# LSH attention and a mixture of experts on one core: who splits the last quarter of the first w1, and how the last chunk is made

## The chip, the cores and the metric

The kernel runs on one NeuronCore of a Trainium2 chip. Its engines work side by side, each through its own queue in order: TensorE (PE; its weight loads are PEld), VectorE (DVE), ScalarE (ACT), GpSimd (POOL) and SyncE (SP), which here only issues transfers. The metric is device time of one execution in microseconds: before the change the median of three runs is 708.36 us (708.22 to 708.40).

## The reference

Attention with a mask from locality-sensitive hashing, over 4 batches of 8 heads with 768 positions of 64 numbers, and then a mixture of 8 experts that sends each of the 3072 tokens to one of them:

```
q_bucket = sum((q @ proj > 0) * 2**arange(6));  k_bucket likewise
scores   = where(q_bucket == k_bucket, q @ k.T / 8, -1e9)
attn     = exp(scores - max) / (sum + 1e-9)
x        = attn @ v                      # as 3072 x 512
e        = argmax(x @ w_gate)            # one expert for a token
h        = relu(x[e] @ w1[e])            # 512 -> 1024
out      = softmax(x @ w_gate)[e] * sigmoid(x @ w_output_gate)[e] * (h @ w2[e])
```

All is float32. To keep its precision on TensorE, operands are split in two parts of the type fp32r, a rounded copy (`hi`) and what the copy leaves (`lo`), and a product is the sum of three matmuls: hi with hi, hi with lo, lo with hi.

## The kernel before

The work has two parts. The **attention part** goes through 192 steps of one tile of scores (128 queries, 768 keys in a folded layout). For a step TensorE makes the scores (line 555), VectorE takes the masked minimum (line 558), ScalarE makes exponentials and their sums (line 566), VectorE the reciprocal for a pair of steps (lines 573 and 574), GpSimd multiplies by it (line 576: the normalisation), TensorE transposes the result in twelve pieces (line 600), ScalarE and VectorE copy these out of PSUM (lines 602 and 606), and TensorE multiplies with v (line 617). A tile is transposed six steps after its scores, so that the engines have time; the last six steps (186 to 191) are transposed in a loop that makes no scores any more.

The **expert part** runs expert after expert, largest first. For an expert, `up` (line 329) makes `h` from gathered tokens, a column block `f` at a time, with ScalarE writing `hh` (line 337) and VectorE `hl` (line 338). Then `h @ w2` is made, for the last experts in rows: `all_rows` makes a chunk of at most 128 tokens by 24 matmuls of 512 columns into one PSUM bank, `ps_m` for even chunks and `ps_a` for odd ones. `send` scales it by the gate into `yo` and scatters its rows to the output with an indirect transfer of GpSimd. The last chunk of the last expert has 96 tokens. For this one `send` lets ScalarE scale the first half of the columns and VectorE the second.

The two parts overlap for the first expert, whose number is known before the last batch ends. Its first 256 tokens are gathered from the batches that are done, turned by TensorE into `ps_m` (a pool with one buffer, lines 279 to 284) and brought out by ScalarE (`xh`, line 283) and VectorE (`xlo`, line 284). Its w1 comes in four quarters of 128x1024 through two buffers named `w_raw`; `early_w1` splits each in two halves on GpSimd (line 938 `hi`, line 939 `lo`). Then eight fills, one for each `f`, are laid among the routing of the last batch; w2 comes in four pieces, two through `w_raw` and two through the idle buffer `pts0`, split by GpSimd (line 179) and VectorE (line 182).

What is issued where is set by tables. `plan(step, fn)` puts `fn` behind the transposes of a step; `late` is step 168, so that the entry 20 for a half of w1 means step 188 and 22 step 190. The queues of TensorE, VectorE, ScalarE and GpSimd follow the order of the program in the two blocks under `manual_schedule`, in the first block SyncE too; where two blocks meet, a scheduler lays small instructions of both between each other. The lines of the table before:

```
for h in range(2):
    plan(late + (8, 10, 13, 14, 16, 19, 20, 22)[2 * cc + h], lambda cc=cc, h=h: early_w1(cc, h))
```

SyncE issues, in this order: the stores of attention rows to `x_dram` (line 636, which wait for VectorE's transposition on line 629), the first two w2 pieces into `w_raw` (line 172, each once that buffer's w1 quarter is split), and the two pieces into `pts0` (line 162).

Of the kernel before, what the change touches and what calls it, by code (L numbers as in the profile page):

```python
# [8 lines left out]
F32 = mybir.dt.float32  # L9
# [4 lines left out]
AF = mybir.ActivationFunctionType  # L14
ALU = mybir.AluOpType
# [9 lines left out]
DM = H * D  # L25
E = 8
# [3 lines left out]
CH = P  # L30
# [13 lines left out]
NCC = DM // P  # L44
GROUP = 2
PER = 6
NFB = F // P
# [7 lines left out]
def f32(ap):  # L55
    return ap.bitcast(F32)
# [3 lines left out]
def lsh_attention_then_moe(  # L60
# [10 lines left out]
    nc = tc.nc  # L71
# [53 lines left out]
    tacc_e, tacc = (cst.tile([CH, 3, E, NCH], F32, name=n) for n in ("tacc_e", "tacc"))  # L125
# [197 lines left out]
    def product(ps, ls, rs, first=True, last=True):  # L323

        pairs = [p for (lh, ll), (rh, rl) in zip(ls, rs) for p in ((lh, rh), (lh, rl), (ll, rh))]
        for k, (l, r) in enumerate(pairs):
            nc.tensor.matmul(ps, l, r, start=first and k == 0, stop=last and k == len(pairs) - 1)  # L327
# [12 lines left out]
    def send(r, a, n, py, sid):  # L340

        yo = mp.tile([CH, DM], F32, name="yo", bufs=4)
        gt = tacc[0:n, 1, r, a:a + 1]
        m = DM // 2 if (r, a) == (E - 1, len(chunks(r)) - 1) else DM
        nc.scalar.activation(yo[0:n, 0:m], py[0:n, 0:m], AF.Copy, scale=gt)  # L345
        if m < DM:
            nc.vector.tensor_scalar(yo[0:n, m:DM], py[0:n, m:DM], gt, None, ALU.mult)
        nc.gpsimd.indirect_dma_start(  # L348
            out=out[:, :], out_offset=bass.IndirectOffsetOnAxis(ap=sid[0:n, r, a:a + 1], axis=0),
            in_=yo[0:n], in_offset=None, bounds_check=NTOK - 1, oob_is_err=False)  # L350
# [25 lines left out]
    def all_rows(r, a, c, n, w2s, hs, sid, between):  # L376
        py = (ps_a if a % 2 else ps_m).tile([CH, DM], F32, name="ps_a" if a % 2 else "ps_m")
        for f in range(0, NFB, 2):
            down_rows(c, n, w2s, hs, py, [f, f + 1])
            between()  # L380
        send(r, a, n, py, sid)

    def chunks(r):

        return [min(CH, CAPS[r] - c) for c in range(0, CAPS[r], CH)]

    with ExitStack() as actx:
# [22 lines left out]
        def plan(step, *fns):  # L410
            at.setdefault(step, []).extend(fns)
# [416 lines left out]
        for b in range(B - 1):  # L828
            r = routing(b)
# [102 lines left out]
        def early_w1(cc, h):  # L932
            if h == 0:
                early.setdefault("w1", []).append(
                    [wpool.tile([P, F], F32R, name="w1" + n, bufs=NCC) for n in "hl"])
            c = slice(h * F // 2, (h + 1) * F // 2)
            hi, lo, raw = (x[:, c] for x in (*early["w1"][cc], early["raw"][cc]))
            nc.gpsimd.tensor_scalar(hi, raw, 1.0, 0.0, ALU.mult, ALU.add)
            nc.gpsimd.tensor_tensor(lo, raw, f32(hi), ALU.subtract)

# [5 lines left out]
        for cc in range(NCC):  # L946
            plan(late + (4, 5, 11, 15)[cc], lambda cc=cc: early_load(cc))
            for h in range(2):
                plan(late + (8, 10, 13, 14, 16, 19, 20, 22)[2 * cc + h], lambda cc=cc, h=h: early_w1(cc, h))

        with tc.manual_schedule(engines=MANUAL | {mybir.EngineType.SP}):
            t = signs()
# [130 lines left out]
    with tc.manual_schedule(engines=MANUAL):  # L1083
# [18 lines left out]
        for r in range(E):  # L1102
# [73 lines left out]
            if n > 3 * CH:  # L1176
                back = [mp.tile([P, 2, CAP], F32, name="yt", bufs=2) for _ in range(NCC // 2)]
                for dp in range(NCC // 2):
                    down(w2s, hs, n, back, dp, between)
            else:  # L1180
                back = None
                c0 = 0 if r else EARLY
                for a in range(c0, len(ch)):
                    all_rows(r, a, a - c0, ch[a], w2s, hs, sid, between)
            split()
            if nxt:
                w1s, xs = w1n, xn
# [109 lines left out]
```

## Time and profile before

| | |
|---|---|
| median of three runs | 708.36 us |
| profiled execution | 708.33 us |
| its span | 706.5 us |
| TensorE busy | 691.4 us, 98% |
| VectorE, ScalarE, GpSimd busy | 466.1, 439.9, 396.7 us |
| chain that ended last | TensorE 91%, VectorE 5% |

Times in the rows below are microseconds from the start of the span. A busy time counts an engine's own instructions; what stands in brackets behind an instruction is the idle time of its engine just before it, and what ended it. Matmuls are pipelined: the duration of one is longer than the distance to the next, and the distance is what counts. An engine that is idle costs something only where another waits for it.

### The profile page before, as it was taken

How to read it: one execution, taken by the hardware profiler on the slowest of the kernel's cores; microseconds unless marked ns; L12 is line 12 of the kernel's file. 1: busy time of each engine (PE TensorE's matmuls, PEld its weight loads, DVE VectorE, ACT ScalarE, POOL GpSimd, SP SyncE). 2: the span in 40 equal slices, each digit the busy share in tenths (PEclk: the TensorE clock that was granted, in tenths of full speed). 3: DMA queues.
4: the chain of work that ended last, by engine and by line, in shares of the span. 5: the costliest groups of instructions: out<-in, count | busy, mean ns of one | idle time of the engine just before them, and what ended most of it. 6: DMA issues, size and time to landing. Idle time of an engine off the chain costs nothing.

```text
span 706.5 us, 17341 instructions
## 1 busy us (share of the span) xinstructions
PE 691.4 (98%) x6591; PEld 543.1 (77%) x6591; DVE 466.1 (66%) x1045; ACT 439.9 (62%) x896; POOL 396.7 (56%) x489
## 2 busy tenths in 40 slices
PE   7999999999999999999999999999999999999996
PEld 4666675767675767675766889889999999989894
DVE  7787887888777888778975944462636455555440
ACT  5789988889788888888887213423425243434231
POOL 6668666575756566656699246344372727474201
PEclk9999999999999999999999999999999999999999
DMA  5544554444444544442535225633454453636401
GB/s 177 142 122 98 122 124 108 116 89 107 116 118 85 117 102 124 86 109 60 144 84 142 54 91 181 218 107 122 163 166 158 163 168 115 215 122 212 152 9 43
DMA packets 85283, 87.47 MB, mean 124 GB/s; under 512 B 57167, under 2 KB 67591, under 8 KB 85192
## 3 DMA queue, kind: packets, MB, share of 16 engines
q1 hardware_dynamic: 79704, 72.88, 37.7%
q0 software_dynamic: 5200, 13.31, 5.5%
q8 instruction: 54, 0.88, 0.5%
q14 instruction: 37, 0.30, 0.2%
q10 hardware_dynamic: 288, 0.10, 0.1%
HBM read 59.57 MB, written 13.11 MB: 103 GB/s over the span
## 4 chain that ended last, share of the span: by engine, by line
PE 91%; DVE 5%; issue 1%; ACT 1%; DMA 1%; POOL 0%; POOLq 0%; DVEq 0%; ACTq 0%
PE ps_s L327 32%; PE ps_a L617 18%; PE ps_s L555 17%; PE ps_t L600 6%; PE ps_m L327 6%; PE ps_a L327 3%; DVE sc L558 2%; PE ps_t L447 1%; PE ps_m L600 1%; PE ps_a L600 1%; PE ps_m L651 1%; PE ps_t L241 1%; DVE w2l L182 1%; PE ps_a L367 0%; PE ps_m L367 0%
## 5 line engine op out<-in xcount | busy, mean ns | idle before, releaser
L576 POOL TENSOR_SCALAR sc<-sc,rsum 128x768 f32<-128x768 f32 x192 | 171.3, 908 | 121.9 <-ACT pts L606 62.9
L558 DVE TENSOR_SCALAR_CACHE_REDUCE sc<-ps_s 128x768 f32<-128x768 f32 x192 | 176.3, 954 | 22.0 <-PE ps_s L555 20.3
L566 ACT ACTIVATE sc<-sc,mn 128x768 f32<-128x768 f32 x192 | 178.8, 951 | 3.7 <-DVE sc L558 3.6
L555 PE MATMUL ps_s<-kh,qhl 64*128 64x384 f32 x768 | 150.5, 404 | 2.3 <-DVE sc L558 1.6
L617 PE MATMUL ps_a<-pts,vt 128*64 128x384 f32 x768 | 131.1, 490 | 0.0
L606 ACT COPY pts<-ps_t 128x384 f32<-128x384 f32 x189 | 93.2, 493 | 34.2 <-PE ps_s L600 27.8
L338 DVE SCALAR_TENSOR_TENSOR hl<-ps_s,hh 128x256 fp32r<-128x256 f32 (+8 forms) x40 | 34.0, 849 | 105.8 <-ACT hh L337 105.8
L617 PEld LDWEIGHTS ps_a<-pts,vt 128*64 128x64 f32 x768 | 52.2, 137 | 66.5 <-issue 61.8
L600 PEld LDWEIGHTS ps_t<-ident,sc 64*128 64x128 f32 x1152 | 83.7, 140 | 20.9 <-POOL sc L576 12.9
L327 PE MATMUL ps_s<-xh,w1h 128*128 128x256 f32 (+7 forms) x288 | 96.8, 336 | 0.0
L327 PE MATMUL ps_s<-xlo,w1h 128*128 128x256 f32 (+7 forms) x288 | 95.3, 331 | 0.0
L348 POOL DMA_INDIRECT out_dram<-yo,sid x29 | 31.0, 1068 | 114.4 <-ACT yo L345 56.8
L327 PE MATMUL ps_s<-xh,w1l 128*128 128x256 f32 (+7 forms) x288 | 95.1, 330 | 0.0
L301 POOL DMA_INDIRECT xq<-x_dram,idx x75 | 81.3, 1084 | 23.8 <-issue 21.1
L600 PE MATMUL ps_t<-ident,sc 64*128 64x64 f32 x1152 | 88.6, 225 | 0.7 <-POOL sc L576 0.7
L337 ACT ACTIVATE hh<-ps_s 128x256 fp32r<-128x256 f32 (+8 forms) x40 | 29.1, 727 | 96.0 <-PE ps_s L327 96.0
L555 PEld LDWEIGHTS ps_s<-kh,qhl 64*128 64x128 f32 x768 | 77.1, 189 | 4.7 <-DVE sc L558 2.8
L555 PE MATMUL ps_s<-bb 64*128 64x384 bf16 x384 | 65.8, 329 | 2.7 <-DVE sc L558 1.6
L555 PE MATMUL ps_s<-kl,qhl 64*128 64x384 f32 x384 | 66.9, 334 | 0.0
L606 ACT COPY pts<-ps_m 128x384 f32<-128x384 f32 x93 | 44.7, 480 | 18.0 <-PE ps_m L600 12.9
L327 PEld LDWEIGHTS ps_s<-xh,w1h 128*128 128x128 f32 x288 | 54.1, 188 | 2.0 <-issue 0.6
L327 PEld LDWEIGHTS ps_s<-xlo,w1h 128*128 128x128 f32 x288 | 54.1, 188 | 1.3 <-DVE xlo L284 0.2
(228 smaller groups left out, 1376.0 us busy)
## 6 DMA issues: line engine op xcount, KB each, us to landing
w_raw<-in_w_dram SPq DMA_DIRECT2D x34, 512.0 KB
qk<-in_qkT_dram SPq DMA_DIRECT2D x32, 384.0 KB
qhl<-qhl SPq DMA_DIRECT2D x62, 192.0 KB
xh<-in_w_dram SPq DMA_DIRECT2D x14, 512.0 KB
xlo<-in_w_dram SPq DMA_DIRECT2D x14, 512.0 KB
vt<-in_v_dram SPq DMA_DIRECT2D x16, 384.0 KB
x_dram<-xb SPq DMA_DIRECT2D x60, 96.0 KB
xq<-x_dram,idx POOLq DMA_INDIRECT x75, 2.8
```

The source lines that it names most:

```text
L301: nc.gpsimd.indirect_dma_start(out=xq[:, k * P:(k + 1) * P], out_offset=None, in_=x_dram.rearrange("n (a f) -> (n a) f", a=NB32), in_offse ...
L327: nc.tensor.matmul(ps, l, r, start=first and k == 0, stop=last and k == len(pairs) - 1)
L337: nc.scalar.activation(hh, ph, AF.Relu)
L338: return lambda: nc.vector.scalar_tensor_tensor(hl, ph, 0.0, f32(hh), ALU.max, ALU.subtract)
L348: nc.gpsimd.indirect_dma_start(out=out[:, :], out_offset=bass.IndirectOffsetOnAxis(ap=sid[0:n, r, a:a + 1], axis=0), in_=yo[0:n], in_offse ...
L555: nc.tensor.matmul(ss[:, h, 0:HS], q[rs, c:c + P], k[rs, 0:HS], start=(i == 0), stop=(i == 3))
L558: nc.vector.tensor_scalar(sc, ss[:, :, 0:HS], MASKED, None, ALU.min, ALU.min, accum_out=mn)
L566: nc.scalar.activation(pr, pr, AF.Exp, bias=mn, scale=-1.0, accum_out=sums[s // GROUP][:, k, 0:1])
L576: nc.gpsimd.tensor_scalar(live[s0 + k], live[s0 + k], rs[:, k:k + 1], 0.0, ALU.mult, ALU.add)
L600: nc.tensor.transpose(trs[h][:, c], pr[r, c * P:(c + 1) * P], ident[r, r])
L606: (nc.vector.tensor_copy if h and (last or s % PER == 0) else nc.scalar.copy)(pts[:, :, t * P + h * hq:t * P + (h + 1) * hq], trs[h])
L617: nc.tensor.matmul(st["av"][j * D:(j + 1) * D], st["v"][:, j, c], blocks[hb][j][:, c], start=(c == 0), stop=(c == NT - 1))
```

## The change

Two things are changed. In `early_w1` the last quarter (`cc == NCC - 1`) is split by VectorE instead of GpSimd, with a copy and a subtraction for each half, and both halves are planned at step 191 (`late + 23`), behind the last step with scores, instead of at 188 and 190. And the last chunk of the last expert is made by a new function, `last_rows`: the two halves of its 512 columns one after the other, the first in `ps_m` and scaled by VectorE, the second in `ps_a` and scaled by ScalarE. The scatter is a function of its own.

```diff
-        m = DM // 2 if (r, a) == (E - 1, len(chunks(r)) - 1) else DM
-        nc.scalar.activation(yo[0:n, 0:m], py[0:n, 0:m], AF.Copy, scale=gt)
-        if m < DM:
-            nc.vector.tensor_scalar(yo[0:n, m:DM], py[0:n, m:DM], gt, None, ALU.mult)
+        nc.scalar.activation(yo[0:n], py[0:n], AF.Copy, scale=gt)
+        scatter(yo, r, a, n, sid)
+
+    def scatter(yo, r, a, n, sid):
+
         nc.gpsimd.indirect_dma_start(
...
+    def last_rows(r, a, c, n, w2s, hs, sid):
+
+        m = DM // 2
+        yo = mp.tile([CH, DM], F32, name="yo", bufs=4)
+        gt = tacc[0:n, 1, r, a:a + 1]
+        cs = slice(c * CH, c * CH + n)
+        for k, (pool, name) in enumerate(((ps_m, "ps_m"), (ps_a, "ps_a"))):
+            py = pool.tile([CH, m], F32, name=name)
+            d = slice(k * m, (k + 1) * m)
+            product(py[0:n], [(hs[0][:, f, cs], hs[1][:, f, cs]) for f in range(NFB)],
+                    [(w2s[f][0][:, d], w2s[f][1][:, d]) for f in range(NFB)])
+            if k == 0:
+                nc.vector.tensor_scalar(yo[0:n, d], py[0:n], gt, None, ALU.mult)
+            else:
+                nc.scalar.activation(yo[0:n, d], py[0:n], AF.Copy, scale=gt)
+        scatter(yo, r, a, n, sid)
...
+            if cc == NCC - 1:
+                nc.vector.tensor_copy(hi, raw)
+                nc.vector.tensor_tensor(lo, raw, f32(hi), ALU.subtract)
+                return
             nc.gpsimd.tensor_scalar(hi, raw, 1.0, 0.0, ALU.mult, ALU.add)
             nc.gpsimd.tensor_tensor(lo, raw, f32(hi), ALU.subtract)
...
-                plan(late + (8, 10, 13, 14, 16, 19, 20, 22)[2 * cc + h], lambda cc=cc, h=h: early_w1(cc, h))
+                plan(late + (8, 10, 13, 14, 16, 19, 23, 23)[2 * cc + h], lambda cc=cc, h=h: early_w1(cc, h))
...
-                    all_rows(r, a, a - c0, ch[a], w2s, hs, sid, between)
+                    if (r, a) == (E - 1, len(ch) - 1):
+                        last_rows(r, a, a - c0, ch[a], w2s, hs, sid)
+                    else:
+                        all_rows(r, a, a - c0, ch[a], w2s, hs, sid, between)
```

What the change does to the queues is seen in their order. First GpSimd at the end of the attention part, before: the normalisations of the last eight steps (`sc`), the gathers of tokens (`xg`), the last three halves of w1 and the copies for w2.

```order
L576 TENSOR_SCALAR sc<-sc,rsum 128x768 x4
L269 DMA xg<-x_dram,gid_7560 128x512 x2
L938 TENSOR_SCALAR w1h<-w_raw 128x512
L939 TENSOR_TENSOR w1l<-w_raw,w1h 128x512
L938 TENSOR_SCALAR w1h<-w_raw 128x512
L939 TENSOR_TENSOR w1l<-w_raw,w1h 128x512
L576 TENSOR_SCALAR sc<-sc,rsum 128x768 x2
L938 TENSOR_SCALAR w1h<-w_raw 128x512
L939 TENSOR_TENSOR w1l<-w_raw,w1h 128x512
L576 TENSOR_SCALAR sc<-sc,rsum 128x768 x4
L179 TENSOR_SCALAR w2h<-w_raw 128x1024 x2
L179 TENSOR_SCALAR w2h<-pts_7869 128x1024 x2
```

And GpSimd in the same place of the changed kernel, whose line numbers are higher by up to 22:

```order
L594 TENSOR_SCALAR sc<-sc,rsum 128x768 x4
L269 DMA xg<-x_dram,gid_7560 128x512 x2
L960 TENSOR_SCALAR w1h<-w_raw 128x512
L961 TENSOR_TENSOR w1l<-w_raw,w1h 128x512
L594 TENSOR_SCALAR sc<-sc,rsum 128x768 x6
L179 TENSOR_SCALAR w2h<-w_raw 128x1024 x2
L179 TENSOR_SCALAR w2h<-pts_7869 128x1024 x2
```

Two halves are gone, and the last six normalisations stand together. Next VectorE in the same place, before: the last four minima (`sc,mn`), the sums and reciprocals of the last three pairs, and the transposition of attention rows (`xb`) between them.

```order
L558 TENSOR_SCALAR sc,mn<-ps_s 128x768 x4
L573 TENSOR_REDUCE rsum<-terms 128x2
L574 RECIPROCAL rsum<-rsum 128x2
L629 STREAM_TRANSPOSE xb<-ot 128x384
L573 TENSOR_REDUCE rsum<-terms 128x2
L574 RECIPROCAL rsum<-rsum 128x2
L573 TENSOR_REDUCE rsum<-terms 128x2
L574 RECIPROCAL rsum<-rsum 128x2
```

The same place on VectorE in the changed kernel:

```order
L576 TENSOR_SCALAR sc,mn<-ps_s 128x768 x4
L591 TENSOR_REDUCE rsum<-terms 128x2
L592 RECIPROCAL rsum<-rsum 128x2
L957 CAST w1h<-w_raw 128x512
L958 TENSOR_TENSOR w1l<-w_raw,w1h 128x512
L957 CAST w1h<-w_raw 128x512
L958 TENSOR_TENSOR w1l<-w_raw,w1h 128x512
L647 STREAM_TRANSPOSE xb<-ot 128x384
L591 TENSOR_REDUCE rsum<-terms 128x2
L592 RECIPROCAL rsum<-rsum 128x2
L591 TENSOR_REDUCE rsum<-terms 128x2
L592 RECIPROCAL rsum<-rsum 128x2
```

The four new instructions stand ahead of the transposition and of the sums of the last two pairs. Third, VectorE later, among the fills: before, from the fifth `hl` to the sixth, with the ranks and places of the last batch (`t_ge`, `t_oa`, `t_na`, `t_pos`, `t_rhs`) and the order of the experts (`perm`, `o_place`, `o_tm`).

```order
L893 SCALAR_TENSOR_TENSOR o_key<-lead,o_key 128x8
L338 SCALAR_TENSOR_TENSOR hl<-ps_s,hh 128x256
L202 TENSOR_TENSOR t_ge<-rank,chki 128x30
L894 TENSOR_TENSOR perm<-o_key 128x64
L205 TENSOR_TENSOR t_oa<-t_ge 128x24
L211 TENSOR_REDUCE t_na<-t_ge 128x6
L897 TENSOR_REDUCE o_place<-perm 128x8
L213 SCALAR_TENSOR_TENSOR t_pos<-t_na,rank 128x6
L226 TENSOR_TENSOR t_rhs<-oneh,t_oa 128x192
L898 TENSOR_TENSOR perm<-o_place,rkdi 128x64
L230 TENSOR_TENSOR t_rhs<-t_rhs,toki 128x192
L230 TENSOR_TENSOR t_rhs<-t_rhs,gate 128x192
```

The instruction behind these is the sixth `hl`. The same place in the changed kernel, from `perm` on, which there stands ahead of the fifth `hl`:

```order
L912 TENSOR_TENSOR perm<-o_key 128x64
L338 SCALAR_TENSOR_TENSOR hl<-ps_s,hh 128x256
L202 TENSOR_TENSOR t_ge<-rank,chki 128x30
L915 TENSOR_REDUCE o_place<-perm 128x8
L205 TENSOR_TENSOR t_oa<-t_ge 128x24
L211 TENSOR_REDUCE t_na<-t_ge 128x6
L916 TENSOR_TENSOR perm<-o_place,rkdi 128x64
L213 SCALAR_TENSOR_TENSOR t_pos<-t_na,rank 128x6
L226 TENSOR_TENSOR t_rhs<-oneh,t_oa 128x192
L933 TENSOR_TENSOR o_tm<-perm,expi 128x64
L230 TENSOR_TENSOR t_rhs<-t_rhs,toki 128x192
L230 TENSOR_TENSOR t_rhs<-t_rhs,gate 128x192
```

The instructions that order the experts stand earlier, and one more of them (`o_tm`) comes ahead of the sixth `hl`. SyncE's queue has the same order as before.

## Rows read from the trace of the kernel before

**Rows 1.** Busy us by stretch (instructions), granted clock, DMA share, GB/s.

```profile
core 0: us, PE busy (x) PEld busy (x) DVE busy (x) ACT busy (x) POOL busy (x), PEclk, DMA share, GB/s
380.00:390.00 10.00, 8.96 (x110) 6.25 (x107) 4.96 (x13) 7.41 (x15) 9.92 (x11) 1.00 0.80 230
...
410.00:700.00 290.00, 290.00 (x1554) 268.50 (x1553) 134.91 (x147) 106.82 (x130) 130.13 (x131) 1.00 0.43 146
```

**Rows 2.** Timeline of GpSimd: start, us, instruction, count, idle before it.

```profile
378.78 0.61 POOL L938 TENSOR_SCALAR w1h<-w_raw 128x512 fp32r<-128x512 f32 x1
...
380.74 1.79 POOL L576 TENSOR_SCALAR sc<-sc,rsum 128x768 f32<-128x768 f32 x2
...
384.46 3.54 POOL L576 TENSOR_SCALAR sc<-sc,rsum 128x768 f32<-128x768 f32 x4
387.98 2.06 POOL L179 TENSOR_SCALAR w2h<-w_raw 128x1024 fp32r<-128x1024 f32 x2
390.80 3.19 POOL L179 TENSOR_SCALAR w2h<-pts 128x1024 fp32r<-128x1024 f32 x2 [0.76 <-DMA pts<-in_w_dram]
```

**Rows 3.** Timeline of TensorE, from the last transposes to the eighth fill.

```profile
382.82 0.79 PE L600 MATMUL ps_t<-ident,sc 64*128 64x64 f32 x12
...
385.42 0.59 PE L600 MATMUL ps_t<-ident,sc 64*128 64x64 f32 x12 [0.74 <-POOL sc L576]
386.30 0.59 PE L600 MATMUL ps_s<-ident,sc 64*128 64x64 f32 x12 [0.29 <-POOL sc L576]
386.81 0.75 PE L281 MATMUL ps_m<-ident,xg 128*128 128x128 f32 x4
...
397.29 0.85 PE L671 MATMUL ps_m<-wgt,ot 128*128 128x32 f32 x6 [0.17 <-DVE ot L620]
...
398.19 0.28 PE L327 MATMUL ps_s<-xlo,w1h 128*128 128x256 f32 x1
...
400.78 0.28 PE L327 MATMUL ps_s<-xh,w1l 128*128 128x256 f32 x1
...
405.61 0.39 PE L327 MATMUL ps_s<-xh,w1h 128*128 128x256 f32 x1
```

**Rows 4.** Timeline of VectorE in the same stretch.

```profile
380.59 0.16 DVE L573 TENSOR_REDUCE rsum<-terms 128x2 f32<-128x4 f32 x1 [2.06 <-ACT sc L566]
...
382.42 0.16 DVE L573 TENSOR_REDUCE rsum<-terms 128x2 f32<-128x4 f32 x1 [1.47 <-ACT sc L566]
...
385.35 0.69 DVE L284 TENSOR_TENSOR xlo<-ps_m,xh 128x512 fp32r<-128x512 f32 x1 [1.14 <-ACT xh L283]
...
389.53 3.55 DVE L182 TENSOR_TENSOR w2l<-w_raw,w2h 128x1024 fp32r<-128x1024 f32 x2
...
396.70 0.54 DVE L620 COPY ot<-ps_a 128x384 f32<-128x384 f32 x1
...
405.13 0.42 DVE L338 SCALAR_TENSOR_TENSOR hl<-ps_s,hh 128x256 fp32r<-128x256 f32 x1
```

**Rows 5.** VectorE's prices: one start, one line by min/median/max, one group.

```profile
4.10 0.35 DVE L472 TENSOR_SCALAR qhl<-qk 64x384 fp32r<-64x384 f32 x1 [1.91 <-DMA qk<-in_qkT_dram]
...
L182 DVE TENSOR_TENSOR w2l<-w_raw,w2h x16: 1216/1222/2054, 389.5 to 679.2; 128x1024 fp32r<-128x1024 f32 x16
...
L510 DVE SCALAR_TENSOR_TENSOR qhl<-qk,qhl 128x384 fp32r<-128x384 f32 x30 | 24.5, 816 | 4.1 <-POOL qhl L504 2.8
```

**Rows 6.** Chain that ended last, merged: start, us, line, pieces.

```profile
695.07 5.54 PE ps_m L327 x24
```

**Rows 7.** Timeline of all engines behind the last product.

```profile
700.68 0.47 ACT L345 ACTIVATE yo<-ps_m,tacc 96x256 f32<-96x256 f32 x1 [4.83 <-PE ps_m L327]
701.18 0.48 DVE L347 TENSOR_SCALAR yo<-ps_m,tacc 96x256 f32<-96x256 f32 x1 [15.53 <-ACT yo L345]
701.94 0.93 POOL L348 DMA_INDIRECT out_dram<-yo,sid  x1 [4.84 <-DVE yo L347]
```

**Rows 8.** Timeline of SyncE's transfers.

```profile
378.56 2.10 SPq L636 DMA_DIRECT2D x_dram<-xb  x4
380.90 0.36 SPq L172 DMA_DIRECT2D w_raw<-in_w_dram  x1
```

## The prediction

> **What bounds the kernel now.** I read three views, in this order. First the busy time by stretch: from 410 to 700 us TensorE is busy 290.00 of 290.00 us at full granted clock [rows 1]. So whatever reaches the end of the attention part earlier is kept to the end, and nothing can be won in that stretch except by taking work off TensorE. Between 380 and 390 us it is busy 8.96 of 10 us, and GpSimd 9.92 [rows 1]: here the attention part runs out and the experts begin. Second, the timelines of the engines in that place, to see who holds TensorE. Third, the tail, where the order of three engines behind the last product is plain.
>
> At the hand-over GpSimd holds TensorE. GpSimd makes a half of the last w1 quarter from 378.78 to 380.74, then two normalisations (1.79 us), then the second half until 384.46, and only then the four last softmax normalisations, 3.54 us for four [rows 2]. TensorE's third set of transposes of the last block starts at 385.42 after 0.74 us of waiting for GpSimd, the fourth at 386.30 after another 0.29 [rows 3]. VectorE, meanwhile, was idle 2.06 us before 380.59 and 1.47 us before 382.42 [rows 4].
>
> **Part one: the last quarter moves from GpSimd to VectorE.** GpSimd loses four instructions, two halves of 1.96 us each (378.78 to 380.74, and as much for the second) [rows 2], 3.9 us in all. VectorE gains four, two copies and two subtractions of 512 columns, between the last minima and the transposition of 0.57 us that started at about 378.0 (380.59 less 2.06 of idle time is 378.53, its end). No row shows a copy of this shape. The nearest is a scaled copy of 384 columns in 0.35 us [rows 5], so 0.47 for 512. A subtraction of 1024 columns takes 1.22 us at the median and 2.05 at most [rows 5]: 0.61 to 1.03 for half of that. The 2.05 were beside GpSimd's copies, which then took 1.60 each instead of 1.03 (3.19 for two against 2.06) [rows 2]. The same addition of 0.42 on a copy makes it 0.9. Four instructions cost VectorE 2.2 us alone and 3.9 us beside a busy GpSimd. GpSimd is busy for the first two thirds of that time, so I take 3.0: from 378.0 to 381.0. The mean of 0.82 us for another two-input instruction of 384 columns [rows 5], 1.09 for 512, agrees with the upper half.
>
> What is queued behind them on VectorE: the transposition of 0.57, then the reduction for the second last pair, which ran at 380.59 [rows 4]. It comes at about 381.6, its reciprocal at about 382.0. GpSimd is free by then (one quarter half and two normalisations from 378.78), and makes four at 0.885: the second last pair by 383.8, the last pair (its reduction at 382.42 [rows 4] is not moved) by 385.5, which was 388.0 before.
>
> TensorE's third set then starts without its 0.74, at 384.68; it lasted 0.59 (386.30 less 0.29 less 385.42), so the fourth is at 385.27, again without a wait, and the second turn of gathered rows is reached at about 385.8. It cannot start there: it writes the one ps_m bank, which the first turn's subtraction on VectorE frees at 385.35 + 0.69 = 386.04 [rows 4]. That subtraction hangs on TensorE and ScalarE, which the change does not move. With 0.05 to the start (as from 397.24 to 397.29 below) the turn begins at 386.09 instead of 386.81 [rows 3]. **Gain here: 0.72 us**, of 1.03 us of waits removed; 0.3 turn into a wait for the bank.
>
> The next place is 397.29: the products that add the last pair of heads to the logits waited 0.17 us for VectorE's copy, 396.70 + 0.54 [rows 3, 4]. That copy is queued behind four subtractions for w2 that began at 389.53 [rows 4]. If TensorE comes 0.72 earlier and VectorE were free, the gain would be 0.72 + 0.17 = 0.89. VectorE's four begin when the last transposes are copied, some 0.6 earlier. If the block keeps its length, 0.6 is all; if it is shorter, because GpSimd's w2 copies are over sooner, up to 0.89. I take 0.75, the middle.
>
> **The order of small instructions behind it.** The code there is the same, but three routing instructions of the expert order come earlier on VectorE: one more stands ahead of the sixth `hl` subtraction, and two dependent ones follow each other closely ahead of the fifth. In the trace the sixth `hl` subtraction ran at 405.13 for 0.42, to 405.55, and TensorE's eighth fill began at 405.61 [rows 3, 4], right behind it, since it takes the PSUM tile that this frees. So any delay there is TensorE's. An instruction of this size with a dependent one beside it is 0.2 to 0.25 us (the small reductions are 0.16 [rows 4], and each waits for the one before). **Cost: 0.25 us**, bounds 0 and 0.4.
>
> **Part two: the tail.** Before, 24 matmuls of 512 columns take 5.54 us [rows 6], then ScalarE scales one half in 0.47 (700.68), then VectorE the other in 0.48 (701.18), having waited for ScalarE, and GpSimd scatters at 701.94 [rows 7]. Afterwards VectorE's half is done while the second half of columns is still in TensorE, so the scatter waits for ScalarE alone: 701.66 less 701.15, 0.51 us saved. TensorE issues 48 matmuls of 256 columns. Such ones stand in the trace 22 steps apart from 398.19 to 400.78 [rows 3], 0.118 us each: 48 make 5.65, 0.11 more than 5.54. Their weights have 96 columns, in that stretch 128, so 0.118 should be no less than what comes. **Gain: 0.40 us** (0.35 to 0.5).
>
> **Sum.** 0.75 - 0.25 + 0.40 = 0.90 us. The profiled execution took 708.33 us, a span of 706.5 and 1.8 around it, and the median of three runs is 708.36. 708.33 - 0.90 = 707.4 us. The likeliest case's own range, with 0.6 to 0.89, 0 to 0.4 and 0.35 to 0.5, is 706.9 to 707.8.
>
> **A rule that speaks against the change.** The rows show VectorE and GpSimd slowing each other when both read SBUF (1.22 to 2.05 and 1.03 to 1.60 us) [rows 2, 5]. The Trainium skill, "SBUF — State Buffer", section "Who interferes with whom", says more: a VectorE copy in its two-port mode, or a VectorE instruction with two SBUF inputs against a GpSimd one that reads SBUF, shares one port pair with it as an exclusive lock, and whoever comes second is blocked until the other has finished. By that rule the new instructions and GpSimd's work add up: VectorE's 2.2, the 0.8 that GpSimd still has of the sixth half at 378.0 and two normalisations of 0.885 are 4.8, so VectorE is free at 382.8, the reciprocal at 383.8; the third set would start at about 384.9 and the turn at 386.3, 0.2 us later than I have it, and the sum would be 0.7.
>
> **The rivals.** *More is won.* The waits of TensorE between 382.82 and 397.29 [rows 3] are 1.20 us in sum. If the bank of the turn comes free sooner than the old rows say, and the shifted order costs nothing, the gain is 0.89 to 1.20 + 0.40, that is 707.0 to 706.7. For it: VectorE's queue has slack in front of the first turn, and the cost of the order is read from one release at 405.55 alone. Against it: the bank's rows hang on TensorE's own start at 382.82 [rows 3].
>
> *Only the tail pays.* If VectorE's block for w2 ends no earlier than before, the wait at 397.29 takes the place of the one at 385.42, and with the order's 0.25 part one is worth nothing or less: 0.40 - 0.25 to 0.40, 708.0 to 708.2. What could hold that block is its input, below. Against it: GpSimd is ready for the w2 copies 2.5 us earlier than at 387.98 [rows 2].
>
> *Slower.* The mechanism is SyncE's queue. Its four stores of attention rows (issued from 378.56 for 2.10 us) wait for VectorE's transposition, and the first w2 load stands behind them, at 380.90 [rows 8]. With the transposition at 381.6 they are issued until 383.7, and the first load comes at 384.0, 3.1 later. The second load was held by its buffer until about 384.5 anyway, which GpSimd freed at 384.46 [rows 2] and VectorE now frees at 381. So all four loads start together at about 384, with the stores still moving. In the trace GpSimd waited for the third piece until 390.80, 0.76 us [rows 2], so there was little slack. If the loads come so late that the last w2 subtraction ends 1.8 us later than before, the 0.40 of the tail is lost and the kernel is 1.4 us slower; from 0.4 us on it is not faster. At 3 us it is 711. Against it: the later loads need no more bytes, the transfer engines were busy only 0.80 of that stretch [rows 1], and the block may slip by 1 us before it costs more than is won. The lock of which the Trainium skill speaks would push it this way, by another 1.8 us on SyncE's stores.
>
> **How the numbers follow.** Chances: the forecast 0.55, more 0.22, only the tail 0.16, slower 0.07. What a measurement of this kernel can tell from no change is about 0.2%, 1.4 us. The forecast and most of the tail case lie inside that; the first rival reaches it only with its best values, and a few tenths that I have not seen would do the rest, so faster is 0.22, same 0.71, slower 0.07. The range, 706.6 to 708.2, takes in all but the far ends of the first rival and the slower one.
>
> **What would show it.** In the profile after: GpSimd's normalisations joined to a group of six with no w1 work between, the last ending near 385.5; no wait for GpSimd at the third and fourth set of transposes, but one of about 0.3 for VectorE or ScalarE at the second turn; the w2 subtractions ending before 395.6; the eighth fill waiting longer for its `hl`; 48 matmuls in about 5.65 us, and only ScalarE between the last of them and the scatter. It is wrong if GpSimd waits over 1.5 us for w2's pieces, if the four VectorE instructions take more than 4 us, or if the narrow matmuls are further apart than 0.12 us.

## The result and the profile after

The changed kernel is slower: 712.52 us, median of four runs (710.33 to 713.0), against 708.29 us for the kernel before (four runs, 706.97 to 708.4) measured beside it. The ratio is 1.0067, with a 95% interval of 1.0054 to 1.0081, that is 3.8 to 5.7 us. The forecast of 707.4 and its range (706.6 to 708.2) missed it, and the case that came had 7% of the chance.

The profiled execution is the fastest of the four: 710.33 us, span 708.6. Its attention part ran earlier from the start: the same products with v (line 635, line 617 before) begin here at 377.56 us, in the trace of before at 378.80. One reason stands in the rows of 10 to 30 us: granted clock 1.00 here, 0.91 there. So times of the hand-over are compared with 1.24 us added to those of the changed kernel.

SyncE after, in the columns of [rows 8]:

```profile
381.23 2.10 SPq L654 DMA_DIRECT2D x_dram<-xb  x4
383.57 1.00 SPq L172 DMA_DIRECT2D w_raw<-in_w_dram  x2
384.83 0.88 SPq L162 DMA_DIRECT2D pts<-in_w_dram  x2
```

The four stores and the first w2 load are each 2.67 us later than in [rows 8], 3.91 with the 1.24. Why the stores are late shows on VectorE (start, length, and in brackets the idle time before):

```profile
376.73 1.11 DVE L957 CAST w1h<-w_raw 128x512 fp32r<-128x512 f32 x1
377.88 1.27 DVE L958 TENSOR_TENSOR w1l<-w_raw,w1h 128x512 fp32r<-128x512 f32 x1
379.07 0.42 DVE L957 CAST w1h<-w_raw 128x512 fp32r<-128x512 f32 x1
379.52 1.19 DVE L958 TENSOR_TENSOR w1l<-w_raw,w1h 128x512 fp32r<-128x512 f32 x1
380.64 0.56 DVE L647 STREAM_TRANSPOSE xb<-ot 128x384 f32<-128x384 f32 x1
...
389.20 1.23 DVE L182 TENSOR_TENSOR w2l<-w_raw,w2h 128x1024 fp32r<-128x1024 f32 x1 [1.40 <-POOL w2h L179]
391.36 1.23 DVE L182 TENSOR_TENSOR w2l<-w_raw,w2h 128x1024 fp32r<-128x1024 f32 x1 [0.94 <-POOL w2h L179]
393.52 3.18 DVE L182 TENSOR_TENSOR w2l<-pts,w2h 128x1024 fp32r<-128x1024 f32 x2 [0.94 <-POOL w2h L179]
...
397.21 0.54 DVE L638 COPY ot<-ps_a 128x384 f32<-128x384 f32 x1
```

The four new instructions take 3.98 us (376.73 to 380.71), and the transposition for which the stores wait stands behind them. In the trace of before it ran here, 3.91 us earlier with the 1.24:

```profile
377.97 0.56 DVE L629 STREAM_TRANSPOSE xb<-ot 128x384 f32<-128x384 f32 x1
```

Further down in the trace of after VectorE waits three times for GpSimd's copies of w2, and the copy that TensorE needs starts at 397.21, 1.75 us later than in [rows 4]. GpSimd itself:

```profile
377.54 2.64 POOL L594 TENSOR_SCALAR sc<-sc,rsum 128x768 f32<-128x768 f32 x2
381.63 3.56 POOL L594 TENSOR_SCALAR sc<-sc,rsum 128x768 f32<-128x768 f32 x4 [1.46 <-DVE rsum L591]
388.12 1.04 POOL L179 TENSOR_SCALAR w2h<-w_raw 128x1024 fp32r<-128x1024 f32 x1 [2.92 <-DMA w_raw<-in_w_dram]
389.89 1.43 POOL L179 TENSOR_SCALAR w2h<-w_raw 128x1024 fp32r<-128x1024 f32 x1 [0.73 <-DMA w_raw<-in_w_dram]
392.07 2.43 POOL L179 TENSOR_SCALAR w2h<-pts 128x1024 fp32r<-128x1024 f32 x2 [0.74 <-DMA pts<-in_w_dram]
```

GpSimd is done with the normalisations at 385.19, with the 1.24 some 1.5 us earlier than in [rows 2], and then waits 2.92 us for the first w2 piece, which lands 4.55 us after its issue (383.57 to 388.12). In [rows 2] the same wait is absent, because GpSimd was still at its own work when that piece landed. The third piece comes late too, though its issue hardly moved. In the trace of before SyncE issued it here:

```profile
385.12 0.88 SPq L162 DMA_DIRECT2D pts<-in_w_dram  x2
```

With the 1.24 it is issued 0.95 us later in the changed kernel (384.83), but GpSimd begins it 2.51 later (392.07 against 390.80 [rows 2]) and ends its last copy 1.75 later. All four loads now move together, right behind the stores: from 382 to 391 us the transfer engines are busy 0.97 of the time, in the trace of before 0.71 (the last column but one; the first line is before).

```profile
382.00:391.00 9.00, 7.96 (x105) 6.07 (x103) 5.63 (x11) 5.79 (x12) 8.15 (x10) 1.00 0.71 236
382.00:391.00 9.00, 8.28 (x108) 6.26 (x109) 4.67 (x8) 4.89 (x9) 5.35 (x6) 1.00 0.97 268
```

And TensorE, from the third set of transposes on:

```profile
383.52 0.59 PE L618 MATMUL ps_t<-ident,sc 64*128 64x64 f32 x12
383.94 0.54 PE L618 MATMUL ps_s<-ident,sc 64*128 64x64 f32 x12
385.02 0.75 PE L281 MATMUL ps_m<-ident,xg 128*128 128x128 f32 x4 [0.54 <-DVE xlo L284]
...
397.80 0.86 PE L689 MATMUL ps_m<-wgt,ot 128*128 128x32 f32 x6 [2.48 <-DVE ot L638]
...
400.17 0.41 PE L327 MATMUL ps_s<-xh,w1h 128*128 128x256 f32 x1
400.39 0.41 PE L327 MATMUL ps_s<-xlo,w1h 128*128 128x256 f32 x1
...
402.92 0.20 PE L745 MATMUL ps_m<-ohb,tri 128*128 128x48 bf16 x1
...
407.59 0.39 PE L327 MATMUL ps_s<-xh,w1h 128*128 128x256 f32 x1
```

The two waits for GpSimd in [rows 3] are gone and the second turn of gathered rows stands 0.55 us earlier. But the last products of the logits wait 2.48 us instead of 0.17 and start 1.75 us later. Behind them the fills run slower: two of their matmuls are 0.22 us apart, in [rows 3] 0.118. The busy times by stretch show it in the last column but two (granted clock):

```profile
398.00:400.00 2.00, 2.00 (x15) 2.00 (x15) 1.28 (x7) 0.00 (x0) 0.00 (x0) 0.74 0.66 97
400.00:402.00 2.00, 2.00 (x11) 2.00 (x11) 1.67 (x8) 0.65 (x3) 0.00 (x0) 0.50 0.03 6
402.00:404.00 2.00, 2.00 (x22) 1.96 (x22) 1.39 (x11) 0.38 (x1) 0.00 (x0) 0.91 0.58 89
```

0.50 is the lower of the clock's two levels, 1.2 instead of 2.4 GHz. The sixteen distances between matmuls from 398.93 to 402.31 are 0.21 on the mean: 1.5 us lost. The ranking product at 402.92 (400.90 before) is 3.26 us late, 1.75 from the wait and 1.5 from the clock; that stays to the end, 3.0 at the last chunk.

The tail:

```profile
696.68 0.28 PE L327 MATMUL ps_m<-w2h,hh 128*96 128x256 f32 x1
...
702.20 0.28 PE L327 MATMUL ps_a<-w2h,hl 128*96 128x256 f32 x1
...
702.57 0.47 ACT L398 ACTIVATE yo<-ps_a,tacc 96x256 f32<-96x256 f32 x1 [4.95 <-PE ps_a L327]
703.31 0.93 POOL L349 DMA_INDIRECT out_dram<-yo,sid  x1 [4.44 <-DVEq L1226]
```

From the first matmul of the last chunk to the scatter it is 6.63 us; in the trace of before it was 7.03, from this matmul to 701.94 [rows 7]:

```profile
694.91 0.39 PE L327 MATMUL ps_m<-w2h,hh 128*96 128x512 f32 x1
```

### The profile page after: what moved, and what is told of

The parts are those of the page before. It is cut to its first block, busy times and chain, and to the rows that moved or that the text cites. A ratio compares the mean times of both kernels' runs of the same rounds, so it can differ in the third digit from the quotient of the medians.

```text
span 708.6 us, 17390 instructions
## 1 busy us (share of the span) xinstructions
PE 691.4 (98%) x6615; PEld 544.9 (77%) x6615; DVE 468.8 (66%) x1049; ACT 439.5 (62%) x896; POOL 394.1 (56%) x485
## 5 line engine op out<-in xcount | busy, mean ns | idle before, releaser
L327 PEld LDWEIGHTS ps_s<-xh,w1l 128*128 128x128 f32 x288 | 54.9, 191 | 1.1
```

## The experiments

Theory A: the w2 loads are late because they stand behind the stores in SyncE's queue, and the stores wait for the transposition. Rivals: the loss is in the narrow matmuls of the tail (B in the first group of runs); VectorE and GpSimd slow each other, wherever the stores are (C). In the last group B is a second part of the cause: behind the wait the granted clock falls. The first four kernels ran on one chip, the next four on another, the last four on a third, each group beside the kernel before (medians 710.85, 708.68 and 708.63 us).

The times in the last three columns are of one profile each, counted from the start of the products with v at 378.80 in before and 377.56 in after: first w2 load issued, last products of the logits, ranking product. The four profiles of the first group have a stop of 0.36 to 0.37 us in TensorE's transposes just ahead of the products with v, which no other profile has; so e1, e3 and e4 are held against e2_tail_only there, whose order up to the tail is that of before, and not against before.

| kernel | median us | ratio to before [95%] | load | logits | ranking |
|---|---|---|---|---|---|
| before | 708.36 | | 2.10 | 18.49 | 22.10 |
| after | 712.52 | 1.0067 [1.0054, 1.0081] | 6.01 | 20.24 | 25.36 |
| e1_split_only | 714.06 | 1.0053 [1.0033, 1.0072] | 6.34 | 20.15 | 23.76 |
| e2_tail_only | 710.21 | 0.9995 [0.9982, 1.0008] | 3.13 | 18.79 | 22.40 |
| e3_rows_first | 709.69 | 0.9986 [0.9974, 0.9999] | 3.13 | 18.70 | 22.31 |
| e4_filler | 712.01 | 1.0019 [1.0005, 1.0033] | 6.35 | 20.40 | 24.00 |
| e5_stores_behind | 707.39 | 0.9983 [0.9969, 0.9996] | 0.03 | 17.61 | 21.17 |
| e6_before_stores_behind | 708.27 | 0.9997 [0.9984, 1.0010] | 0.02 | 18.51 | 22.12 |
| e8_before_rows_late | 708.98 | 1.0011 [0.9997, 1.0026] | 5.00 | 19.33 | 22.83 |
| e7_both | 707.27 | 0.9977 [0.9965, 0.9989] | 0.03 | 17.40 | 20.89 |
| e9_changed_again | 710.82 | 1.0038 [1.0023, 1.0053] | 6.02 | 20.33 | 23.93 |
| e10_wait | 711.72 | 1.0036 [1.0022, 1.0050] | 0.04 | 19.92 | 26.47 |
| e11_wait_filler | 709.94 | 1.0016 [1.0004, 1.0028] | 0.03 | 19.93 | 23.54 |
| e12_filler_again | 709.62 | 1.0009 [0.9996, 1.0023] | 6.02 | 20.57 | 24.18 |

**One part alone.** e1_split_only gives the tail back (`send` scales in two halves again, not shown):

```diff
...
-                    if (r, a) == (E - 1, len(ch) - 1):
-                        last_rows(r, a, a - c0, ch[a], w2s, hs, sid)
-                    else:
-                        all_rows(r, a, a - c0, ch[a], w2s, hs, sid, between)
+                    all_rows(r, a, a - c0, ch[a], w2s, hs, sid, between)
```

> The split of the last w1 quarter on VectorE alone; the last chunk is made as before the change. Theory A (SyncE's queue: the four VectorE instructions push back the transposition of attention rows, its stores, and the w2 loads behind them; TensorE waits for the w2 split and its clock falls): the tail gave 0.4 us, so this is 0.4 us slower than the changed kernel, 712.9 us, against 708.3 before; the wait ahead of the last logits is 2.5 us again. Theory B (the 48 narrow matmuls of the tail cost the time): as fast as before or faster, 707.5 to 708.3.

e2_tail_only gives the split back:

```diff
-            if cc == NCC - 1:
-                nc.vector.tensor_copy(hi, raw)
-                nc.vector.tensor_tensor(lo, raw, f32(hi), ALU.subtract)
-                return
...
-                plan(late + (8, 10, 13, 14, 16, 19, 23, 23)[2 * cc + h], lambda cc=cc, h=h: early_w1(cc, h))
+                plan(late + (8, 10, 13, 14, 16, 19, 20, 22)[2 * cc + h], lambda cc=cc, h=h: early_w1(cc, h))
```

> The tail alone: the last chunk in two halves of columns, the split left to GpSimd at its old steps. Theory A: 0.4 us faster than before, 707.9 us, with the scatter 0.51 us nearer to the last matmul and the 48 matmuls 0.1 us longer than the 24. Theory B: the time of the changed kernel, 712 us.

The split alone costs 3.8 us (ratio 1.0053), the tail alone nothing that can be told from none (0.9995). The loss is in the split; the tail is cleared. In e1's profile the wait at the logits is 2.11 us and the granted clock behind it 1.00, so the clock does not fall every time.

**The order on VectorE.** e3_rows_first keeps the split on VectorE, but behind the transposition:

```diff
-                plan(late + (8, 10, 13, 14, 16, 19, 23, 23)[2 * cc + h], lambda cc=cc, h=h: early_w1(cc, h))
+                if cc == NCC - 1:
+                    block(late + 24, "early", lambda cc=cc, h=h: early_w1(cc, h))
+                    continue
+                plan(late + (8, 10, 13, 14, 16, 19)[2 * cc + h], lambda cc=cc, h=h: early_w1(cc, h))
```

> The changed kernel with one thing moved: the four VectorE instructions stand behind the transposition of attention rows and ahead of the sums of the second last pair; VectorE has the same work and GpSimd too. Theory A: the stores are issued at their old time, the first w2 load 2.6 us earlier than in the changed kernel, the wait ahead of the last logits is under 0.3 us and the clock stays full: 707.2 us (0.55 us won at the transposes, 0.17 at the logits, 0.4 in the tail). Theory C (VectorE and GpSimd hold each other up over SBUF, or the normalisations come late): the four instructions cost the same 4 us at the same place, so the time stays near the changed kernel's, above 711 us.

Its SyncE, and the product that waited:

```profile
378.69 2.11 SPq L654 DMA_DIRECT2D x_dram<-xb  x4
381.04 1.29 SPq L172 DMA_DIRECT2D w_raw<-in_w_dram  x2
```

```profile
396.61 0.85 PE L689 MATMUL ps_m<-wgt,ot 128*128 128x32 f32 x6 [0.56 <-DVE ot L638]
```

The first load is issued as early as in e2_tail_only (3.13 us in the table), the wait is 0.56 us (expected: under 0.3), and the kernel is by its interval just faster than before. The same four instructions on the same engine, moved past one instruction of 0.56 us, no longer cost anything that shows. C in its plain form falls. But the split wins next to nothing here either: the logits come 0.09 us earlier than in e2_tail_only (18.70 and 18.79), where GpSimd has it, and the ratios of the two (0.9986 and 0.9995) are not told apart.

**The order on SyncE.** e5_stores_behind leaves the change as it is and lets SyncE issue the stores behind the four w2 loads; e6_before_stores_behind does the same to the kernel before:

```diff
+        held = []
...
-            for a in range(4):
-                nc.sync.dma_start(xv[:, ts, i * P + 32 * a:i * P + 32 * (a + 1)], st["xb"][32 * a:32 * (a + 1), ts])
+            def stores():
+                for a in range(4):
+                    nc.sync.dma_start(xv[:, ts, i * P + 32 * a:i * P + 32 * (a + 1)], st["xb"][32 * a:32 * (a + 1), ts])
+            if g == NP - 2:
+                held.append(stores)
+            else:
+                stores()
...
                 w2s += w2_piece(ep, 0, f, "h", raw)
+            held.pop(0)()
```

> The changed kernel, with one edit: SyncE issues the four stores of the second last pair's attention rows behind the four w2 loads, so that no load stands behind VectorE's late transposition. VectorE's and GpSimd's order is the changed kernel's. Theory A (SyncE's queue: the loads are late because they stand behind the stores) expects the first w2 load about 2.5 us earlier than in the changed kernel's profile, GpSimd's 2.92 us wait for w_raw and TensorE's 2.48 us wait for VectorE's copy (line 638 there) gone or below 0.8 us, no fall of the granted clock, and 0 to 1.5 us less than the kernel before (ratio 0.998 to 1.000). Theory C (VectorE and GpSimd slow each other, wherever the stores are) expects what the change took: about 4 us more than before (ratio 1.005).

> The kernel before, with the same edit alone: the four stores behind the four w2 loads. It tells what the order of SyncE is worth by itself. In the kernel before the second w2 load waits for its buffer anyway, so theory A expects little: GpSimd's wait for the third piece (0.76 us) gone and the wait at the logits (0.17 us) with it, 0 to 0.3 us less than before. If the ratio is below 0.998, then what the next kernels win is the order of SyncE and not the split.

SyncE, GpSimd and TensorE of e5_stores_behind:

```profile
380.81 3.49 SPq L172 DMA_DIRECT2D w_raw<-in_w_dram  x2
385.00 0.88 SPq L162 DMA_DIRECT2D pts<-in_w_dram  x2
385.99 6.64 SPq L657 DMA_DIRECT2D x_dram<-xb  x4
```

```profile
388.38 2.08 POOL L179 TENSOR_SCALAR w2h<-w_raw 128x1024 fp32r<-128x1024 f32 x2
391.41 3.62 POOL L179 TENSOR_SCALAR w2h<-pts 128x1024 fp32r<-128x1024 f32 x2 [0.96 <-DMA pts<-in_w_dram]
```

```profile
398.39 0.80 PE L697 MATMUL ps_m<-wgt,ot 128*128 128x32 f32 x6
```

VectorE's transposition is as late as in the changed kernel, yet GpSimd finds the first two pieces ready (it waits 0.96 us for the third) and TensorE does not wait at all; the time falls from 2 to 4 us above before (the two groups with the changed kernel) to 1.2 below. That is theory A, shown by taking the link between stores and loads away. e6 (0.9997) says that the new order of SyncE is worth nothing in the kernel before: its wait at the logits is 0.23 us, as before, since there GpSimd's own work sets the copies.

**The link in the kernel before.** e8_before_rows_late only moves the transposition behind the sums of its pair:

```diff
-                    block(12 * g + 6 * hf + 3 * PER, "early", lambda g=g, hf=hf: rows(g, hf))
+                    when = "amid" if (g, hf) == (NP - 2, 1) else "early"
+                    block(12 * g + 6 * hf + 3 * PER, when, lambda g=g, hf=hf: rows(g, hf))
```

> The kernel before, with VectorE's transposition of the second last pair's attention rows moved behind the sums of that pair, some 2.5 us later; nothing is added to VectorE, and GpSimd keeps the split of all four quarters. Theory A expects the stores and with them the first w2 load 2 to 3 us later on SyncE, a wait of GpSimd for w_raw of 1 to 2 us, a wait of TensorE for VectorE's copy at the logits of 1 to 2.5 us, and 1 to 3.5 us more than before (ratio 1.0015 to 1.005). Theory C, by which only the added VectorE work beside GpSimd costs, expects no change (ratio 0.9995 to 1.0005).

```profile
397.44 0.85 PE L671 MATMUL ps_m<-wgt,ot 128*128 128x32 f32 x6 [1.06 <-DVE ot L620]
```

The wait comes (1.06 us, 0.17 before), with nothing added to VectorE, but the time is not told from before (1.0011, interval 0.9997 to 1.0026), below what I expected. The profiles give the size: the load is 2.90 us later than before and the logits 0.84; in the changed kernel 3.91 and 1.75. Both differences are 2.1 (further down, in e9 2.1 and in e12 1.8): by these profiles so much of a late first load stays hidden, and the rest arrives at TensorE. It does not arrive by the first piece alone. The third piece:

```profile
384.42 0.88 SPq L162 DMA_DIRECT2D pts<-in_w_dram  x2
```

```profile
391.72 2.41 POOL L179 TENSOR_SCALAR w2h<-pts 128x1024 fp32r<-128x1024 f32 x2 [0.76 <-DMA pts<-in_w_dram]
```

Counted from the products with v (378.11 here), it is issued at 6.31, as in the kernel before (6.32), but GpSimd gets it at 13.61 instead of 12.00. So stores and a first load that are issued late make a load behind them land late that was issued in time. An estimate fits: the 512 KB of one load more in front of it take 1.5 us at the 339 GB/s that the trace of before shows from 386 to 390 us.

**Both orders.** e7_both joins the edits of e3 and e5.

> The changed kernel with VectorE's four new instructions placed behind the transposition of attention rows (as in e3_rows_first) and the four stores behind the w2 loads. Theory A expects the loads no later than before, so that the 0.4 us of the tail and 0.6 to 0.9 us of the hand-over stand: 1.0 to 1.6 us less than the kernel before (ratio 0.9977 to 0.9986), 0 to 0.6 us better than e3_rows_first. Theory C expects as much as e3_rows_first (ratio 0.9986) and no more.

```profile
397.27 0.85 PE L697 MATMUL ps_m<-wgt,ot 128*128 128x32 f32 x6
```

0.9977: 1.6 us faster than before, the best of all, with no wait at the logits. Over e3 it is 0.9 in a thousand, as A expects, though e3's interval reaches to 0.9974, and e5 alone is nearly as good.

**The clock.** e9_changed_again is the changed kernel once more; e12_filler_again (and e4_filler, in the first group) gives TensorE 18 transposes of a constant ahead of the product that waits:

```diff
             fill(1)
+            idle = ps_t.tile([P, 3, P], F32, name="ps_t")
+            for i in range(18):
+                nc.tensor.transpose(idle[:, i % 3], ident, ident)
```

e10_wait is e7_both with VectorE's last subtractions repeated, which makes the wait without touching SyncE; e11_wait_filler has the transposes as well:

```diff
+            for _ in range(2):
+                for j in range(2):
+                    nc.vector.tensor_tensor(w2s[NFB - 2 + j][1], raw[:, j], f32(w2s[NFB - 2 + j][0]), ALU.subtract)
```

> The changed kernel with 18 idle transposes of the identity (2.5 us at full clock) put on TensorE where it waits for the last logits; nothing reads them. If part of the loss is the clock that falls behind that wait (measured: 0.50 granted from 400 to 402 us), the wait stays but the fills behind it run at full clock: 1.5 us less than the profiled run of the changed kernel, some 1.5 to 3 us less in the median, 709.5 to 711 us. If the clock is not the cause of a part, 712.5 us or more.

> The changed kernel itself, once more, beside the next three on one chip. Expected: 3 to 4.5 us more than the kernel before (ratio 1.0045 to 1.0065), a wait of TensorE for VectorE's copy (line 638) of about 2.5 us, and behind it, if theory B (the granted clock falls behind a wait of that length) holds in general, a stretch of some 2 to 4 us at a granted clock of 0.5 to 0.8; if this profile shows 1.00 there, the fall is not bound to the wait.

> e7_both, which has no wait at the logits, with the subtractions of the last w2 piece repeated twice on VectorE (four instructions of 512 columns, about 2.7 us, the same result), ahead of the copy that TensorE waits for. SyncE's order, GpSimd and the split are those of e7_both. If only the length of the wait counts (theory A alone), this costs about 2.5 us over e7_both, 0.9 to 1.5 us more than the kernel before (ratio 1.001 to 1.002). If a wait of this length also brings the clock down (theory B), it costs 4 to 5 us over e7_both, 2.5 to 3.5 us more than before (ratio 1.0035 to 1.005), with a granted clock below 0.9 in the 4 us behind it.

> e10_wait with 18 transposes of a constant on TensorE ahead of the product that waits, results not used, about 2 us of work that fills most of the wait. Theory A alone expects the same time as e10_wait (within 0.3 us), since TensorE only works where it would wait. Theory B expects the granted clock at 1.00 behind it and 1.5 to 2.5 us less than e10_wait.

> The changed kernel with the same 18 transposes ahead of the last products of the logits (e4_filler again, now beside the changed kernel itself). Theory B expects 1.5 to 3 us less than e9_changed_again and a granted clock of 1.00 behind the wait; theory A alone expects the same as e9_changed_again.

e10_wait, TensorE and the busy times behind it:

```profile
397.32 1.46 PE L697 MATMUL ps_m<-wgt,ot 128*128 128x32 f32 x6 [2.36 <-DVE ot L639]
```

```profile
396.00:398.00 2.00, 0.68 (x4) 0.68 (x4) 1.60 (x5) 0.00 (x0) 0.00 (x0) 0.84 0.16 25
398.00:400.00 2.00, 2.00 (x10) 2.00 (x11) 1.07 (x6) 0.00 (x0) 0.00 (x0) 0.50 0.50 74
400.00:402.00 2.00, 2.00 (x12) 2.00 (x11) 1.30 (x6) 0.46 (x3) 0.00 (x0) 0.50 0.01 4
402.00:404.00 2.00, 2.00 (x13) 1.91 (x13) 1.41 (x9) 0.19 (x2) 0.00 (x0) 0.50 0.62 95
```

The same of e11_wait_filler:

```profile
397.25 0.86 PE L697 MATMUL ps_m<-wgt,ot 128*128 128x32 f32 x6 [0.35 <-DVE ot L639]
```

```profile
398.00:400.00 2.00, 2.00 (x18) 2.00 (x18) 1.67 (x8) 0.36 (x2) 0.00 (x0) 1.00 0.50 74
400.00:402.00 2.00, 2.00 (x24) 1.96 (x23) 1.92 (x11) 0.67 (x4) 0.00 (x0) 1.00 0.21 37
```

And of e9_changed_again:

```profile
399.49 0.85 PE L689 MATMUL ps_m<-wgt,ot 128*128 128x32 f32 x6 [2.62 <-DVE ot L638]
```

```profile
400.00:402.00 2.00, 2.00 (x19) 2.00 (x19) 1.46 (x7) 0.12 (x1) 0.00 (x0) 1.00 0.57 84
```

In e10 and e11 the logits come at the same time (19.92 and 19.93 us in the table), and the ranking product 2.93 us later where nothing filled the wait. By the ratios the filler is worth 1.4 us there (1.0036 and 1.0016) and 2.1 on the changed kernel (1.0038 and 1.0009); in the first group e4_filler has 1.0019 and e1_split_only, without filler and without the 0.4 us of the tail, 1.0053. The profiles of e4, e11 and e12 show 1.00 behind the wait. Work that nobody uses makes the kernel faster; where the profiles show why, it is the clock. But e9's own profile, with a wait of 2.62 us, keeps 1.00. So B holds on the mean and not in every execution: the mean granted clock of e9's runs is 0.9947, of before's in that group 0.9976, of e12's 0.9972; of e10's 0.9948, of e11's 0.9969. Times the span, an estimate, that is 2.1 us of full clock that e9 loses against before, of which the filler gives back 1.8 in e12, and 1.5 in e11 against e10. Such a mean counts every fall in an execution, also those that have nothing to do with this wait: from 20 to 30 us the profile of before has 0.87, that of e9 0.84. The size by the times is the weak point: the intervals of e9 and e12 touch, and those of e10 and e11 overlap. The changed kernel cost 4.2 us at first (four runs) and 2.2 in this group (twelve runs, 0.0038 by the ratio, 2.7 us), less than expected. In how many executions the clock falls behind the wait was not measured. It does not explain that difference: the mean clock of the first four runs, 0.9942, is close to e9's. The difference stays open.

## Why the prediction was wrong, step by step

**The step that failed** is "VectorE's four begin when the last transposes are copied, some 0.6 earlier". The w2 block does not begin when VectorE is free, but when its input is there. It ended 1.75 us later, not 0.6 earlier. The text named the mechanism as its slower rival, down to "the last w2 subtraction ends 1.8 us later than before", and gave it 0.07. Against it stood that the loads "need no more bytes", which says nothing of when they are issued, nor of how long each takes when all move at once (transfer engines busy 0.97 of the time from 382 to 391 us); and that "GpSimd is ready for the w2 copies 2.5 us earlier" was read as room, where an engine that is ready earlier for a load that comes later waits the longer. The rows held two terms of the sum: load at 380.90 [rows 8], work of GpSimd that covers it until 387.98 [rows 2]. With 4.55 us from issue to landing, which the trace of after gives (in before the transfers stand still from 384.5 to 385.0, so there it took at most 3.6), 2.5 us of cover were left (2.1, read at the logits), against a delay that the text itself put at 3.1 us. The excess alone, 0.6 to 1.0 us, takes the 0.75 of part one away and turns it into a loss. Nor was the 0.75 there with the load at its old place: in e3 the logits gain 0.09 us on e2. GpSimd, free earlier, then waits 1.32 us for the second piece. The split alone (e3) and earlier loads alone (e6) win nothing at the logits; both together (e7) win 1.09 us. Of the signs that the text named for its being wrong, "GpSimd waits over 1.5 us for w2's pieces" is the one that came.

**VectorE's four instructions** were taken at 3.0 us, with 2.2 and 3.9 as bounds; they took 3.98, so the delay was 3.91 and not 3.1. The Trainium skill, "SBUF — State Buffer", section "Who interferes with whom", would, if it held for all of these instructions, let VectorE and GpSimd take strict turns: from 376.73 the 0.83 us that GpSimd's subtraction still had, two normalisations of 0.9 and VectorE's 2.2 make 4.8, until 381.6. Measured was 380.71, and GpSimd's two took 2.64 instead of 1.79 [rows 2]. So they slow each other by about what my upper bound said, and 0.9 us less than by strict turns.

**The clock** was not in the sum at all. It cost 1.5 us in the profiled execution. The Trainium skill, "TensorE: Matmul & The Clock Gate", section "HAM oscillation — how this bites in real kernels", describes, for waits for data that are longer than those here, how TensorE starts its next work at the lower clock; the traces of after and of e10_wait show the same behind 2.48 and 2.36 us (0.50), that of e9_changed_again does not (1.00 behind 2.62).

**What was right.** The waits of 0.74 and 0.29 us are gone, and a wait for the bank of the gathered rows takes their place (0.54 us, expected 0.3); the turn comes 0.55 us earlier, expected 0.72. Where the loads are issued earlier than before (e7: 0.03 us in the table instead of 2.10), the gain is there and more: in e7's profile the turn is 0.71 us earlier than before, and the logits 1.09. The tail gave 0.40 us, as worked out, with 48 matmuls 0.1175 us apart.

**The order of small instructions** cost nothing: the eighth fill is 4.67 us behind the ranking product (407.59 less 402.92), before 4.71 (405.61 less 400.90). The three instructions that came earlier did not delay the release; why not was not tried.

## What to carry to other kernels

When an instruction is delayed, follow every queue that waits for it to its end, also one that only issues transfers: four stores that waited for one transposition held back a load that has nothing to do with them. Price that load by its time from issue to landing, beside the transfers that will then move with it, against the cover it has left, and remember that freeing its consumer shrinks the cover and wins nothing where the load sets the pace. And price a long wait of TensorE above its length, since the clock may fall behind it.

## What was not expected of the hardware

The granted clock of 0.50 behind a single wait of about 2.4 us, in some executions only (after and e10_wait; not e1, e9). A subtraction of 512 columns on VectorE took 0.69 us where GpSimd stood idle (the second in e3) and 1.19 to 1.27 beside GpSimd's work; a copy took 0.42 or 1.11, both beside GpSimd's work. From the last scatter's issue to the end of the span the profiles show 4.3 (e3) to 5.8 us (e7), which is noise larger than the tail's gain: before has 4.56, after 5.29.
